# One function pass on ScalarE for the MLP's activation, a masked product on the first attention level, and weights converted in four wide VectorE instructions

## The chip, the core and the metric

The kernel runs on one core of a Trainium2 chip. The core has a matrix engine (TensorE, PE in the profile; PEld is its weight load), a vector engine (VectorE, DVE), a function engine (ScalarE, ACT), GpSimd (POOL) and SyncE (SP), which issues the DMAs. Each engine works through its own queue in order; semaphores join them. The metric is the device time of one execution in microseconds (us).

## The reference

A gated linear recurrence over 768 tokens (4 batches, 8 heads, head size 48), and an MLP on its output with a quick GELU:

```python
for t in range(S):
    state = f[:, :, t, :, None] * state + np.einsum('bhd,bhe->bhde', k[:, :, t], v[:, :, t])
    y[:, :, t] = np.einsum('bhd,bhde->bhe', q[:, :, t], state)
...
h = x @ w_in                                   # (3072, 384) @ (384, 2048)
g = h * (1.0 / (1.0 + np.exp(-1.702 * h)))
return (g @ w_out).astype(np.float32)          # (3072, 2048) @ (2048, 384)
```

with f = sigmoid(f_logit). q, k, v and f_logit are float32. The two weight matrices come as float64, 12.6 MB together, so each weight reaches the kernel as two 32-bit words.

## The kernel before, in words

**Units.** The 3072 tokens are cut into 12 units of 256 (three to a batch). Each unit is computed in its attention part (chunks of 64 tokens, six levels inside a chunk) and, some time later, in its MLP part. Everything is float32.

**Attention, level by level.** TensorE writes the scores of level l into one PSUM tile `sc` (there is a single buffer of it). VectorE then multiplies the slots X by decay products in place (`promote`, L469 in units 0 to 2, L473 later), ScalarE copies the next level's keys (`Kc`, L444, in `set_aside`), and VectorE moves the scores that the level's mask admits out of PSUM into A by a predicated copy (`evacuate`, L437). The next level's scores need that copy of the keys and a free `sc`. After six levels come the transposed keys (`tkn`, `kn`), the product with v (L484), the state update on VectorE (`st`, L590 and L591) and the product with the states (L612), whose result ScalarE copies (`yT`, L622) and a DMA rearranges into xT, the MLP's input. From unit 3 on two levels go together.

**Decay.** The sigmoid of f_logit is F. In units 0 to 2 TensorE transposes the raw input and ScalarE applies the sigmoid on the way out of PSUM (L355). From unit 3 on VectorE transposes it in two halves (L338) and ScalarE applies the sigmoid to each half in place (L343). GpSimd multiplies F up into `tot`.

**MLP.** For each of 16 column blocks ff, six matrix records (three contractions, each in two passes) make h in one of four PSUM buffers of tag `mm`. ScalarE writes sg = sigmoid(1.702 h) (L784), VectorE writes g = h * sg (L785), which frees the buffer. Units 0 to 2 multiply g by w_out in groups of four blocks (L807, added up in `sum` on VectorE, L845); later units use seven products over quarters (L756).

**Weights.** A pair is two pieces of 128x384 weights, 16 pairs in all. `fetch_weights` loads a pair as 32-bit words (`bits`, three buffers); `begin_pair` has ScalarE scale the high words of each piece (L215) and queues five VectorE instructions for each piece: shift (L230), sign (L226), mask (L233), multiply by the low words (L234) and add (L235). `convert` emits one of them at a time. `merge` spreads these calls over the attention parts of units 0 to 3 in a proportion to each part's kind, and puts the MLP's matmuls between the attention's on TensorE; a matmul is not emitted until its weights' conversion has been emitted. A pair's buffer is fetched into again when the pair is done.

**What sets the order.** TensorE's queue is written out by hand throughout, the other engines' as well up to unit 3 (`fill_order`); later a scheduler places their instructions by its own costs. Loads of ScalarE's function table are put in by the compiler, ahead of an instruction whose function the loaded table lacks.

Of the kernel before, what the change touches and what calls it, by code (L numbers as in the profile page):

```python
# [23 lines left out]
def kernel(  # L24
# [131 lines left out]
    pieces, pairs = [], []  # L156
    for r in range(NGR):
# [10 lines left out]
        pieces += [w_in[:, :, ff * P:(ff + 1) * P] for ff in ffs] + [w_out[:, ff, :] for ff in ffs]  # L168
    NPC = 2 * FG
    NOP = 5  # L170
# [3 lines left out]
    def fetch_weights():  # L174
# [13 lines left out]
        by_dst = by_dst.rearrange("p c (f two) -> p c f two", two=2)  # L188
        if dst.shape[1] == NK:
            fetched[2 * n], fetched[2 * n + 1] = by_dst[:, :, :P], by_dst[:, :, P:]  # L190
        else:
            fetched[2 * n], fetched[2 * n + 1] = by_dst[:, 0], by_dst[:, 1]

    def begin_pair(m):

        chains = []
        for n in (2 * m, 2 * m + 1):
            if n not in fetched:  # L200
                continue
            dst = pieces[n]
            bits = fetched.pop(n)
            at = (slice(None),) * (len(dst.shape))
            lo, hi = bits[at + (0,)], bits[at + (1,)]

            def tmp(tag, bufs, n=n, dst=dst):
                t = wp.tile([P, DM], F32, tag=tag, name=f"{tag}_{n}", bufs=bufs)
                return t.rearrange("p (c f) -> p c f", c=NK) if len(dst.shape) == 3 else t[:]

            a = tmp("a", 4)
            nc.scalar.activation(a, hi.bitcast(F32), AF.Copy, scale=2.0 ** -112)  # L215
            chains.append(chain(dst, lo, hi, a, tmp))
        for ops in zip(*chains):
            todo.extend(ops)
        todo.append(None)

    def chain(dst, lo, hi, a, tmp):
        ve, ai, t = nc.vector, a.bitcast(I32), {}

        def sign():
            t["s"] = tmp("s", 2)
            ve.scalar_tensor_tensor(  # L226
                t["s"].bitcast(I32), hi, -(1 << 31), ai, op0=ALU.bitwise_and, op1=ALU.bitwise_or
            )
        return (
            lambda: ve.tensor_scalar(ai, ai, 3, None, op0=ALU.logical_shift_left),  # L230
            sign,

# [5 lines left out]
    def convert():  # L238

        if state["begin"] < len(pairs) and len(todo) <= NOP:  # L240
            begin_pair(state["begin"])
            state["begin"] += 1
# [71 lines left out]
    def attention(n):  # L314
# [176 lines left out]
        def level(l):  # L491
# [4 lines left out]
            if l == 2:  # L496
                reverse_v(n)
# [506 lines left out]
```

## Time and profile before

| | |
|---|---|
| median of 8 runs | 644.19 us (642.36 to 646.5) |
| profiled execution, its own time | 644.63 us |
| its span in the profile | 642.9 us |
| TensorE busy | 607.8 us, 95% |
| VectorE busy | 475.4 us, 74% |
| ScalarE busy | 240.5 us, 37% |
| mean granted TensorE clock | 0.973 |
| ScalarE table loads | 1 |

The profile shows one execution. 1.7 us of its time lie outside the span. Busy shares are means over stages with different limits: the attention of units 0 and 1 (up to about 92 us) has little MLP work to fill TensorE with, the later units have much. A row of the profile names the source line, the engine, the operation and output<-input; a bracket at a row's end tells how long the engine had been idle and what ended that.

### The profile page before, as it was taken

To read this page: it belongs to the slowest core of one execution; us is meant where nothing else is said; L and a number is where in the kernel's file an instruction comes from. 1 tells how busy PE (TensorE), PEld (TensorE's weight loads), DVE (VectorE), ACT (ScalarE), POOL (GpSimd) and SP (SyncE) were. 2 spreads that over 40 slices of the span, in tenths; PEclk is the share of its full clock that TensorE was granted. 3 is DMA by queue.
4 is the path that set the end of the run, shared out by engine and by line. 5 is a ranking of instruction groups with operands and counts; after the bars stand their busy time and mean duration, and the time that the engine had idled before them with its cause. 6 is when DMAs were issued, how large, how long until landed. Compare 5 with 4: busy or idle time off the path is not lost.

```text
span 642.9 us, 17439 instructions
## 1 busy us (share of the span) xinstructions
PE 607.8 (95%) x7302; PEld 522.0 (81%) x7302; DVE 475.4 (74%) x915; ACT 240.5 (37%) x552; POOL 38.7 (6%) x93
## 2 busy tenths in 40 slices
PE   5877789988999999999999999999999999999997
PEld 5466467665676778988989988988989989989996
DVE  0896999878988877687777787777698776652671
ACT  3254462253413424434524434434344253233120
POOL 4001020002000100100001001001001001000000
PEclk8676999998999999999999999999999999999999
DMA  6874772365004345344434334443232120101000
GB/s 147 222 163 104 197 176 79 88 167 119 1 1 131 93 115 127 84 100 122 105 104 98 87 92 106 107 116 91 62 102 69 51 66 21 33 1 26 25 2 25
DMA packets 83251, 58.23 MB, mean 91 GB/s; under 512 B 33573, under 2 KB 75205, under 8 KB 83173
## 3 DMA queue, kind: packets, MB, share of 16 engines
q1 hardware_dynamic: 83173, 57.12, 35.0%
q8 instruction: 57, 0.93, 0.6%
q14 instruction: 21, 0.17, 0.1%
HBM read 43.98 MB, written 8.39 MB: 81 GB/s over the span
## 4 chain that ended last, share of the span: by engine, by line
PE 76%; DVE 11%; DMA 4%; SPq 3%; ACT 3%; issue 2%; DVEq 0%; ACTq 0%
PE h L779 33%; PE o_X L756 8%; PE o_Y L756 8%; PE o_Z L756 7%; PE o L807 7%; PE sc L395 5%; PE o_W L756 4%; DMA raw<-in_q_dram 2%; PE sc L572 2%; PE y L612 1%; DMA bits<-in_moe_w_out_dram 1%; DVE A L437 1%; DVE X L473 1%; DVE s L226 1%; DVE g L785 1%
## 5 line engine op out<-in xcount | busy, mean ns | idle before, releaser
L779 PE MATMUL h<-xT,w_in 128*128 128x256 f32 (+1 forms) x1152 | 259.9, 384 | 3.6 <-ACT kn L529 1.7
L779 PEld LDWEIGHTS h<-xT,w_in 128*128 128x128 f32 x1152 | 218.2, 191 | 35.8 <-ACT kn L529 2.0
L784 ACT ACTIVATE sg<-h 128x256 f32<-128x256 f32 (+1 forms) x192 | 72.4, 384 | 163.9 <-PE h L779 155.2
L785 DVE TENSOR_TENSOR g<-h,sg 128x256 f32<-128x256 f32 (+1 forms) x192 | 79.5, 420 | 50.3 <-ACT sg L784 49.3
L444 ACT COPY Kc<-X 128x512 f32<-128x512 f32 x72 | 48.1, 668 | 104.3 <-DVE X L473 56.7
L473 DVE TENSOR_TENSOR X<-X,tot 128x1024 f32<-128x1024 f32 x45 | 55.0, 1222 | 30.2 <-PE sc L395 25.8
L807 PE MATMUL o<-w_out,g 128*128 128x384 f32 x192 | 67.1, 497 | 0.9 <-DVE g L785 0.9
L437 DVE COPY_PREDICATED A<-masks,sc 128x256 f32<-128x256 uint32 (+1 forms) x120 | 66.3, 610 | 0.1
L807 PEld LDWEIGHTS o<-w_out,g 128*128 128x128 f32 x192 | 35.7, 193 | 23.5 <-DVE g L785 2.2
L756 PE MATMUL o_X<-w_out,g 128*128 128x192 f32 x288 | 52.6, 331 | 0.0
L756 PE MATMUL o_Y<-T,S 128*128 128x192 f32 x288 | 51.7, 329 | 0.0
L756 PEld LDWEIGHTS o_Y<-T,S 128*128 128x128 f32 x288 | 47.0, 190 | 1.1 <-issue 0.7
L756 PEld LDWEIGHTS o_X<-w_out,g 128*128 128x128 f32 x288 | 46.7, 190 | 1.0
L395 PEld LDWEIGHTS sc<-X,Kc 48*64 48x64 f32 x1440 | 27.4, 141 | 21.9 <-ACT Kc L444 15.6
L395 PE MATMUL sc<-X,Kc 48*64 48x64 f32 x1440 | 32.2, 228 | 13.2 <-ACT Kc L444 7.2
L386 POOL TENSOR_TENSOR tot<-F 128x512 f32<-128x512 f32 x12 | 12.5, 1041 | 494.5 <-DVE st L590 430.5
L622 ACT COPY yT<-y 48x256 f32<-48x256 f32 x96 | 35.2, 367 | 16.8 <-PE y L612 15.6
L338 DVE STREAM_TRANSPOSE X<-raw 128x512 f32<-128x512 f32 x36 | 38.5, 1092 | 0.0
L350 PE MATMUL t<-ident,raw 128*64 128x128 f32 x288 | 22.0, 319 | 6.5 <-POOL ones L143 4.4
L701 DVE TENSOR_TENSOR g<-g,S 128x512 f32<-128x512 f32 x18 | 12.6, 702 | 18.4 <-PE o_X L756 18.4
L350 PEld LDWEIGHTS t<-ident,raw 128*64 128x64 f32 x288 | 19.9, 164 | 7.8 <-POOL ones L143 4.4
L756 PE MATMUL o_Z<-T,g 128*128 128x192 f32 x144 | 24.9, 326 | 0.0
(85 smaller groups left out, 649.2 us busy)
## 6 DMA issues: line engine op xcount, KB each, us to landing
bits<-in_moe_w_out_dram SPq DMA_DIRECT2D x8, 768.0 KB
raw<-in_f_logit_dram SPq DMA_DIRECT2D x48, 96.0 KB
raw<-in_k_dram SPq DMA_DIRECT2D x48, 96.0 KB
bits<-in_moe_w_in_dram SPq DMA_DIRECT2D x8, 576.0 KB
raw<-in_q_dram SPq DMA_DIRECT2D x47, 96.0 KB
k_tok<-z SPq DMA_DIRECT2D x56, 64.0 KB
kt<-k_tok SPq DMA_DIRECT2D x14, 256.0 KB
xT<-yT SPq DMA_DIRECT2D x24, 144.0 KB
```

What stands on the lines that cost most here:

```text
L338: nc.vector.transpose(view(out, at, [[HALF, NP], [step, R4], [R4 * step, 32]]), by_half[:, j, f].rearrange("p a (j d) -> p (a j) d", j=R4) ...
L350: nc.tensor.matmul(pt[h * HS:(h + 1) * HS, jj, :], lhsT=by_pair[j][:, h, x:x + HS], rhs=ident, start=True, stop=True)
L395: nc.tensor.matmul(t["sc"][g * HS:(g + 1) * HS, h, a, s, :], lhsT=t["Kc", l][rows(h), x:x + HS], rhs=rhs(h, a, g), start=True, stop=True,)
L437: nc.vector.copy_predicated(out=view(A, at, dims), mask=mask.bitcast(U32), data=got)
L444: nc.scalar.copy(c.rearrange("p (n two m) -> p n two m", two=2, m=m), view(X, KF * SLOT, [[2 * m, SLOT // (2 * m)], [(KR - KF) * SLOT + m, ...
L473: nc.vector.tensor_tensor(x, x, y, ALU.mult)
L622: nc.scalar.copy(view(yT[rows(h)], at, [[U, NP], [step, HS]]), py[columns(h, g), g, :, f, :])
L756: nc.tensor.matmul(t[bank], lhsT=lhs(f), rhs=rhs(f), start=(new and f == 0), stop=(f == HF - 1), skip_group_check=True,)
L779: nc.tensor.matmul(ph, lhsT=w_in[:, c, ff * P:(ff + 1) * P], rhs=xTs[n][:, c, :], start=(c == 0), stop=(c == NK - 1))
L784: nc.scalar.activation(sg, ph, AF.Sigmoid, scale=1.702)
L785: nc.vector.tensor_tensor(g[ff // FG][:, ff % FG, :], ph, sg, ALU.mult)
L807: nc.tensor.matmul(t["po"], lhsT=g[ff // FG][:, ff % FG, tt * P:(tt + 1) * P], rhs=w_out[:, ff, :], start=(ff == ffs[0]), stop=(ff == ffs[ ...
```

## The change

1. **g in one pass.** `mlp_h` calls one ScalarE function, Gelu_apprx_sigmoid (x times the sigmoid of 1.702 x), from PSUM straight to g. The tile sg and VectorE's 192 products L785 are gone.
2. **The sigmoid of the decay in one instruction.** The function of the MLP and the sigmoid lie in different tables, and the program now has 22 table loads where it had one. From unit 3 on one sigmoid covers both halves of F, after both transposes; in unit 2 the PSUM copies are plain and one sigmoid over F follows.
3. **First level.** `evacuate` writes level 1's scores into A as a product with the 0/1 mask (all positions of that level, zeros too) in place of the predicated copy.
4. **Weights by pairs.** ScalarE scales both pieces in one pass with Prelu, whose negative slope of -2^32 leaves the sign in place, so that the sign instruction is gone; VectorE has four instructions of 128x768 for a pair in place of ten of 128x384. The counts in `merge` are halved in proportion. The pair's scratch s has one buffer (a has two).
5. Unit 0 reverses v after level 4 and not after level 2; the tile T4 takes two buffers of 128x768 in place of four of 128x384.

```diff
-            a = tmp("a", 4)
-            nc.scalar.activation(a, hi.bitcast(F32), AF.Copy, scale=2.0 ** -112)
-        return (
-            lambda: ve.tensor_scalar(ai, ai, 3, None, op0=ALU.logical_shift_left),
-            sign,
-            lambda: ve.tensor_scalar(ai, t["s"].bitcast(I32), -(1 << 23), None, op0=ALU.bitwise_and),
-            lambda: ve.scalar_tensor_tensor(a, lo.bitcast(U32), 2.0 ** -52, a, op0=ALU.mult, op1=ALU.mult),
-            lambda: ve.tensor_tensor(dst, a, t["s"], ALU.add),
-        )
+        a, s = tmp("a", 2), tmp("s", 1)
+        ai, si = a.bitcast(I32), s.bitcast(I32)
+        nc.scalar.activation(a, hi.bitcast(F32), AF.Prelu, scale=2.0 ** -112, alpha=-(2.0 ** 32))
+        todo.extend((
+            lambda: ve.tensor_scalar(si, ai, 3, None, op0=ALU.logical_shift_left),
+            lambda: ve.tensor_scalar(ai, si, -(1 << 23), None, op0=ALU.bitwise_and),
+            lambda: ve.scalar_tensor_tensor(a, lo.bitcast(U32), 2.0 ** -52, a, op0=ALU.mult, op1=ALU.mult),
+            lambda: ve.tensor_tensor(dst, a, s, ALU.add),
+            None,
+        ))
...
-                    if fn:
-                        nc.scalar.activation(out, out, fn)
+                if fn:
+                    nc.scalar.activation(F, F, fn)
...
-                        pt.rearrange("p j (a f i) -> p f a i j", a=NP, f=2)[:, 1 - f], fn or AF.Copy,
+                        pt.rearrange("p j (a f i) -> p f a i j", a=NP, f=2)[:, 1 - f],
+                        fn if fn and n < N_FILL - 1 else AF.Copy,
                     )
+            if fn and n == N_FILL - 1:
+                nc.scalar.activation(F, F, fn)
...
+                if m == 1:
+                    nc.vector.tensor_tensor(
+                        view(A, 0, [[HALF, 2 * NP], [HS + 1, 2], [2, 32]]),
+                        t["sc"].rearrange("p h a s (f t) -> p (h a) s f t", f=2)[:, :, s],
+                        masks[:, l].unsqueeze(1).broadcast_to((P, 2 * NP, 2, 32)), ALU.mult,
+                    )
+                    continue
...
-                sg = mlp.tile([P, width(n)], F32, tag="sg", name=f"sg_{n}_{ff}")
-                nc.scalar.activation(sg, ph, AF.Sigmoid, scale=1.702)
-                nc.vector.tensor_tensor(g[ff // FG][:, ff % FG, :], ph, sg, ALU.mult)
+                nc.scalar.activation(g[ff // FG][:, ff % FG, :], ph, AF.Gelu_apprx_sigmoid)
...
-            n_ops = min(int(pieces * NOP * at_ops / (by * total_ops)), pieces * NOP) - ops
+            most = pieces * NOP // 2
+            n_ops = min(int(most * at_ops / (by * total_ops)), most) - ops
```

TensorE's queue holds the same matmuls in the same order. Three places where the others' order matters:

VectorE, unit 1, from the promotion of level 3 to that of level 4 (`X<-X,tot`; `a_`, `s_`, `bits_` and `w_` belong to the conversion, `g_` is the MLP's product), before and changed:

```order
L469 TENSOR_TENSOR X<-X,tot_621 128x2x32x8 x2
L437 COPY_PREDICATED A<-masks,sc_13_824 128x8x4x8 x2
L230 TENSOR_SCALAR a_815<-a_815 128x384
L785 TENSOR_TENSOR g_0_759<-h_3_848,sg_3_852 128x256
L226 SCALAR_TENSOR_TENSOR s_855<-bits_497,a_813 128x384
L226 SCALAR_TENSOR_TENSOR s_857<-bits_497,a_815 128x384
L233 TENSOR_SCALAR a_813<-s_855 128x384
L233 TENSOR_SCALAR a_815<-s_857 128x384
L234 SCALAR_TENSOR_TENSOR a_813<-bits_497,a_813 128x384
L234 SCALAR_TENSOR_TENSOR a_815<-bits_497,a_815 128x384
L235 TENSOR_TENSOR w_in<-a_813,s_855 128x3x128
L469 TENSOR_TENSOR X<-X,tot_621 128x2x16x16 x2
```

```order
L454 TENSOR_TENSOR X<-X,tot_589 128x2x32x8 x2
L422 COPY_PREDICATED A<-masks,sc_13_771 128x8x4x8 x2
L206 TENSOR_SCALAR s_766<-a_765 128x768
L207 TENSOR_SCALAR a_765<-s_766 128x768
L208 SCALAR_TENSOR_TENSOR a_765<-bits_469,a_765 128x768
L209 TENSOR_TENSOR w_in<-a_765,s_766 128x3x256
L454 TENSOR_TENSOR X<-X,tot_589 128x2x16x16 x2
```

Between the two promotions eight conversion instructions and a product became four wide instructions.

ScalarE where unit 3's decay meets the MLP blocks of units 0 and 1 (`F` the decay, `h_` the MLP's PSUM tiles, `kn_` the copies of the transposed keys), before and changed:

```order
L784 ACTIVATE sg_10_1519<-h_10_1515 128x256
L343 ACTIVATE F<-F 128x512 x2
L215 ACTIVATE a_1544<-bits_1365 128x384
L215 ACTIVATE a_1546<-bits_1365 128x384
L784 ACTIVATE sg_11_1553<-h_11_1549 128x256
L529 COPY kn_1557<-tkn_0_1558 128x512
```

```order
L768 ACTIVATE g_8_1362<-h_10_1374 128x256
L318 ACT_TABLE_LOAD
L318 ACTIVATE F<-F 128x1024
L768 ACT_TABLE_LOAD
L768 ACTIVATE g_8_1362<-h_11_1401 128x256
L514 COPY kn_1406<-tkn_0_1407 128x512
```

Two table loads stand around the sigmoid, ahead of block 11 and of the copy of kn; the scaling pass of the conversion moved behind that copy. The first load's wait is for VectorE's transposes of F; the second waits for nothing.

ScalarE in the units after, shown for one (`p_3`, `osb` the copies of the seven products' banks, `yT` the attention's output):

```order
L705 COPY p_3_2545<-o_X 128x192
L318 ACT_TABLE_LOAD
L318 ACTIVATE F<-F 128x1024
L708 COPY p_3_2573<-o_W 128x192
L607 COPY yT_2611<-y_2447 48x4x64 x8
L429 COPY Kc_2_2661<-X 128x512
```

The same instructions stood in this order before, with two sigmoids of 128x512 in place of the one and no load. The load that brings the MLP's function back stands behind the copy Kc of the last level and ahead of the next unit's first block of h.

More of the change, by code (lines that the diff above doesn't have):

```diff
@@ L153 @@
     NGR = NFF // FG
-    pieces, pairs = [], []
+    pairs = []
     for r in range(NGR):
@@ L167 @@
                 (lambda t: t[:], moe_w_out[ff * P:(ff + 2) * P, :].rearrange("(c p) f -> p c f", c=2))]))
-        pieces += [w_in[:, :, ff * P:(ff + 1) * P] for ff in ffs] + [w_out[:, ff, :] for ff in ffs]
     NPC = 2 * FG
-    NOP = 5
+    NOP = 4
     fetched, todo = {}, []
@@ L950 @@
         fn()
-    for _ in range(4):
+    for _ in range(2):
         convert()
```

46 lines of the change are left out of this document (14 added, 32 removed).

## The prediction

> **What bounds the kernel now.** I read the page's slices first (the granted clock's row, 40 slices of 16 us), then the busy times by stage (one column each: stage, length, busy PE, PEld, DVE, ACT and POOL, granted clock, DMA share, GB/s), cut where the attention of units 0, 1 and 2 ends.
>
> ```profile
> span 642.9 us, 17439 instructions
> PEclk8676999998999999999999999999999999999999
> 17.50:51.60 34.10, 25.81 (x510) 19.44 (x503) 28.89 (x65) 14.77 (x36) 2.82 (x6) 0.75 0.78 188
> 51.60:92.20 40.60, 32.91 (x541) 24.64 (x539) 37.57 (x88) 17.28 (x42) 1.04 (x1) 0.87 0.62 159
> 92.20:129.00 36.80, 36.80 (x288) 26.52 (x289) 32.44 (x72) 13.07 (x32) 2.44 (x5) 1.00 0.35 91
> 129.00:175.00 46.00, 41.06 (x453) 29.96 (x452) 39.79 (x77) 19.36 (x44) 3.24 (x6) 0.96 0.41 100
> 175.00:562.00 387.00, 384.72 (x4810) 341.79 (x4809) 298.04 (x530) 150.62 (x336) 22.57 (x48) 1.00 0.34 86
> ```
>
> There are two kernels here. From 92 us on TensorE sets the pace: 36.80 of 36.80 us busy at full clock, later 384.72 of 387.00. Work taken off VectorE there can win back TensorE's idle time and no more. Before 92 us TensorE idles and runs at 0.75 and 0.87 of its clock, while VectorE is busy for 28.89 of 34.10 and 37.57 of 40.60 us. There VectorE's own work is the path. What TensorE waits for later, from the table of waits (us in total, times, longest; the first three rows of 92 to 175 us, the last of 175 to 643):
>
> ```profile
> PE h L779 <- ACT kn L529: 1.7, 1, 1.7
> PE h L779 <- DVE sum L845: 1.2, 1, 1.2
> PE o L807 <- DVE g L785: 0.9, 1, 0.9
> PE sc L572 <- ACT kn L551: 2.3, 5, 0.5
> ```
>
> **The change, part by part.** VectorE's timeline in units 0 and 1, with one row of TensorE's (57.03):
>
> ```profile
> 17.58 0.81 DVE L230 TENSOR_SCALAR a<-a 128x384 int32<-128x384 int32 x2 [12.81 <-ACT a L215]
> 19.24 1.42 DVE L469 TENSOR_TENSOR X<-X,F 128x512 f32<-128x512 f32 x2
> 20.57 1.29 DVE L437 COPY_PREDICATED A<-masks,sc 128x512 f32<-128x512 uint32 x1
> ...
> 38.58 1.29 DVE L469 TENSOR_TENSOR X<-X,tot 128x512 f32<-128x512 f32 x2
> ...
> 51.67 1.42 DVE L469 TENSOR_TENSOR X<-X,F 128x512 f32<-128x512 f32 x2 [3.76 <-ACT yT L622]
> ...
> 57.03 5.46 PE L779 MATMUL h<-xT,w_in 128*128 128x256 f32 x12 [0.69 <-DMA xT<-yT]
> 63.55 1.41 DVE L469 TENSOR_TENSOR X<-X,tot 128x512 f32<-128x512 f32 x2
> ...
> 82.48 0.62 DVE L230 TENSOR_SCALAR a<-a 128x384 int32<-128x384 int32 x2
> 83.01 1.02 DVE L226 SCALAR_TENSOR_TENSOR s<-bits,a 128x384 int32<-128x384 int32 x2
> 83.95 0.62 DVE L233 TENSOR_SCALAR a<-s 128x384 int32<-128x384 int32 x2
> 84.49 1.02 DVE L234 SCALAR_TENSOR_TENSOR a<-bits,a 128x384 f32<-128x384 uint32 x2
> 85.43 0.55 DVE L235 TENSOR_TENSOR w_out<-a,s 128x384 f32<-128x384 f32 x1
> 85.89 0.42 DVE L785 TENSOR_TENSOR g<-h,sg 128x256 f32<-128x256 f32 x1
> 86.23 0.55 DVE L235 TENSOR_TENSOR w_out<-a,s 128x384 f32<-128x384 f32 x1
> ...
> 163.69 0.96 DVE L673 TENSOR_TENSOR T<-w_out 128x768 f32<-128x768 f32 x1
> 164.57 0.42 DVE L785 TENSOR_TENSOR g<-h,sg 128x256 f32<-128x256 f32 x1
> ```
>
> *A pair's price.* Durations overlap by some 0.08 us, so I take starts. The old pair costs 83.01-82.48 = 0.53, then 0.94, 0.54, 0.94 and twice 0.46: 3.87 us. The new one has a multiply and an add of 128x768, each 0.88 by the sum of that size at 163.69 (the next starts at 164.57), and two TENSOR_SCALARs of 128x768. Two of half the size step 0.53 us; one instruction pays the fixed part once, so between 0.45 and 0.53; I take 0.50. New pair 2.76, saved 1.1 us.
>
> *The product g* gives 0.34 us of VectorE each (85.89 to 86.23). *Level 1's evacuation* took 1.29 us (20.57). A product with a PSUM operand costs 0.42 at 256 columns and 0.55 at 384 (L785, L845 below), so some 0.68 at 512: 0.6 saved per unit; bounds 0 and 0.7.
>
> ```profile
> L785 DVE TENSOR_TENSOR g<-h,sg 128x256 f32<-128x256 f32 (+1 forms) x192 | 79.5, 420 | 50.3 <-ACT sg L784 49.3
> L845 DVE TENSOR_TENSOR sum<-sum,o 128x384 f32<-128x384 f32 x18 | 9.9, 551 | 2.7 <-PE o L807 2.5
> L784 ACT ACTIVATE sg<-h 128x256 f32<-128x256 f32 (+1 forms) x192 | 72.4, 384 | 163.9 <-PE h L779 155.2
> L215 ACT ACTIVATE a<-bits 128x384 f32<-128x384 f32 x32 | 16.2, 557 | 1.6 <-DMA bits<-in_moe_w_in_dram 0.8 <-DVE w_out L235 0.8
> ```
>
> *Unit 0, to the last promotion at 38.58.* Level follows level as promotion, evacuation (there is one sc), scores on TensorE; conversions longer than those scores push the next promotion back. Up to there VectorE has 23 conversion instructions, 8.7 us by the prices above; in the new order nine, 6.1 us (five TENSOR_SCALARs, four wide ones). With the evacuation's 0.6 this gives 3.2 us. From 38.58 to 51.67 TensorE and ScalarE carry the path (VectorE ends by waiting 3.76 us for yT), so nothing more.
>
> *Unit 1.* Five pairs 5.5, six products 2.0, the evacuation 0.6: 8.1 us. Not all of it counts: the promotion at 63.55 waits for scores that stand behind two blocks of h, which start when xT has landed and run at half clock (57.03, 5.46 us); VectorE's work in that hole, some 2.5 us, is hidden already. I take 5.5. Front together 8.7 us. Bounds: 3.2 if unit 1 hangs wholly on xT, ScalarE and DMA; 11.3 if nothing is hidden.
>
> *92 to 129 us:* TensorE is full, 0. *129 to 175 us:* TensorE idles 46.00-41.06 = 4.9 us and loses 0.04 of its clock, 1.8 us. Each releaser is VectorE, or the copy kn, which stands on ScalarE behind the sigmoid of F, which waits for VectorE's transposes. Three and a half pairs (3.9 us) and some 20 products (6.8 us) leave VectorE there. I take 3 of the 6.7; bounds 0 and 6.7. *After 175 us:* all the idle time is the 2.3 us for kn, late because ScalarE, ahead of it, waited for VectorE to give a buffer of sg back (298.64 below, with kn behind it); that buffer is gone. I take 2.
>
> *ScalarE.* The pass over h stays as it is, one of 0.38 us (only the table differs). One scaling pass of 768 columns in place of two of 384 saves a fixed part; nothing waits for it. The new cost is 21 table loads:
>
> ```profile
> 0.73 1.28 ACT L355 ACT_TABLE_LOAD   x1 [0.73 <-PEq L988]
> ...
> 298.64 0.39 ACT L784 ACTIVATE sg<-h 128x256 f32<-128x256 f32 x1 [0.79 <-DVE g L785]
> 298.92 1.12 ACT L551 COPY kn<-kt 128x512 f32<-128x512 f32 x1
> ...
> 306.98 0.63 ACT L343 ACTIVATE F<-F 128x512 f32<-128x512 f32 x1 [0.33 <-DVE F L338]
> 309.10 3.04 ACT L622 COPY yT<-y 48x256 f32<-48x256 f32 x8 [1.28 <-PE y L612]
> 322.34 0.62 ACT L444 COPY Kc<-X 128x512 f32<-128x512 f32 x1 [1.42 <-DVE X L473]
> 324.43 0.38 ACT L784 ACTIVATE sg<-h 128x256 f32<-128x256 f32 x1 [1.48 <-PE h L779]
> 326.71 18.40 PE L779 MATMUL h<-xT,w_in 128*128 128x256 f32 x84
> ...
> 340.11 1.23 DVE L473 TENSOR_TENSOR X<-X,F 128x1024 f32<-128x1024 f32 x1 [1.23 <-ACT Qc L450]
> ```
>
> At 1.28 us each that is 27 us of an engine that waits 155 us for h. In the later units the first load and the wider sigmoid (1.1 us, as 256 columns take 0.38 and 512 take 0.63) end 1.8 us later than the old ones; the 1.28 us of waiting before yT (309.10) covers most of it, and F itself is first read at 340.11. The second load fits into the 1.48 us before the next h (324.43). In units 4 and 5 the sigmoid stands among the h blocks; TensorE makes one in 1.31 us (six of the 84 records at 326.71), so four buffers hold 5.2 us against 3.7. Cost there 0; without that cover 1.3 us a load. In unit 3, where kn is waited for, two loads (2.6 us) stand in the path. There the transposes lose a conversion and products ahead of them and come some 2 to 3 us earlier, so I let them cancel, and the 1.7 us of that wait stays; that is why I take 3, not 6.7.
>
> The Trainium skill speaks against this part: "ScalarE: Activation LUTs", section "What ACT_TABLE_LOAD costs", gives 1283 ns for the load, as the row has it, and about 1380 ns more for a drain, 2.66 us per switch, which no row here shows. By it unit 3's pair is 2.8 us longer and, as an estimate, the sum below 11 instead of 13.7 us.
>
> **Sum.** 3.2 + 5.5 + 3 + 2 = 13.7 us off the profiled execution's 644.63 us (span 642.9 and 1.7 around it): 630.9 us. That execution was 0.4 us above the median of 644.19, so I say 630.5 us for a median.
>
> **The rivals.** *A: the front is held by something else.* Before 92 us DMA moves 188 and 159 GB/s, 12.9 MB in 75 us; in 66 us it would have to move 195, and each pair's load waits for the conversion three pairs before. If transfers or xT take over, half of unit 0 and unit 1 is left, 4 us, and 1 later: 639.5 us. Against it: ScalarE's scaling waits only 0.8 us for bits now. *B: more than the sum.* Unit 1 gives all of its 8.1 us; a denser TensorE gets its full clock before the two blocks at 57.03 (2.6 instead of 5.46 us, by the records at 326.71); the later part gives the 5 us of the sum. 11.3 + 2.9 + 5 = 19.2, so 625.5 us. For it speaks that the clock is full from 64 us on, when the matmuls become dense. In the Trainium skill, "TensorE: Matmul & The Clock Gate", Part 1, the gate opens after about 3.4 us of sustained work; the row of the clock agrees in kind, and whether earlier density moves it no row can tell. *C, slower: the switches are exposed.* If at each of the nine sigmoids from unit 3 on the pair of loads and the sigmoid (2 x 1.28 + 1.1 us) stop the release of h's four PSUM buffers, TensorE, which fills one every 1.3 us, waits up to 3.7 us a unit: 33 us, 664 us. It decides from 1.5 us a unit (13.7 over nine). Against it: in six of the nine the sigmoid stands between the seven products, where no h is being made, and the h buffers come free earlier without VectorE's product. *D: the function's pass takes longer than the sigmoid's.* Even doubled, 0.77 us is under the 1.3 us that TensorE takes for a block; it would cost next to nothing.
>
> **How the numbers follow.** The forecast 61%, A 20%, B 12%, C 7% (D changes none of them). A measurement of this kernel tells 0.3%, 1.9 us, from no change. C in its full form is slower by more; a partial C falls among the forecast and A. So faster 0.88 (forecast, B and nearly all of A), same 0.05, slower 0.07. The forecast's own range is 626 to 636: front 3.2 to 11.3, later 0 to 9, not both at an end. For 8 in 10 I go up to A: 625 to 640.
>
> **What would show it.** After: VectorE near 370 us busy (475 less 80 for g, 18 for the pairs and 7 for level 1), ScalarE near 265. Right: the promotion that opened unit 1 at 51.67 stands near 48.5, unit 2's stage opens near 83.5 (now 92.2), TensorE full from there on. A would show as scaling passes or h waiting for DMA before 80 us. C as idle time of h ended by ScalarE in each unit. The forecast is wrong if TensorE's idle time behind 85 us is above 8 us, or if the front shrinks by under 4 us.

## The result and the profile after

The changed kernel takes 630.16 us (median of 11 runs, 624.64 to 633.05) against 644.78 us before (32 runs beside it): a ratio of 0.9763, 95% interval 0.9738 to 0.9788. The forecast of 630.5 us stands, but several of its terms do not. Executions of one kernel spread with the mean granted clock: the changed kernel took 624.64 to 627.55 us at 0.995 and 632.85 and 633.05 us at 0.983.

The page of the changed kernel (busy times; the granted clock in 40 slices of 15.7 us; the chain by engine):

```profile
span 628.8 us, 17045 instructions
PE 598.1 (95%) x7302; PEld 517.0 (82%) x7302; DVE 383.6 (61%) x625; ACT 263.8 (42%) x549; POOL 41.2 (7%) x93
PEclk8987999999999999999999999999999999999999
PE 87%; DVE 4%; ACT 2%; issue 2%; DMA 2%; SPq 2%; DVEq 0%; ACTq 0%
```

VectorE lost 92 us of work and the span 14.1 us; ScalarE gained 23 us of busy time and is on 2% of the chain. To see where the 14.1 us come from, I cut both executions at the same instructions, VectorE's promotions and TensorE's h blocks. Columns: stretch, length, busy PE, PEld, DVE, ACT and POOL (with counts), granted clock, DMA share, GB/s. First the kernel before: unit 0's promotions, unit 1's first three, from there to unit 2, unit 3 between two of TensorE's records, and the rest:

```profile
19.24:38.58 19.34, 14.23 (x234) 9.38 (x233) 18.57 (x41) 7.52 (x18) 0.00 (x0) 0.76 0.73 201
...
51.67:63.55 11.88, 10.44 (x110) 8.24 (x107) 9.94 (x20) 4.27 (x10) 0.00 (x0) 0.57 0.34 82
63.55:92.29 28.74, 22.48 (x432) 16.41 (x432) 27.62 (x69) 13.03 (x31) 1.11 (x2) 1.00 0.73 191
...
133.99:178.28 44.29, 41.07 (x442) 28.98 (x443) 38.34 (x77) 16.68 (x38) 3.24 (x6) 0.96 0.39 94
178.28:643.00 464.72, 458.56 (x5403) 410.98 (x5402) 332.01 (x600) 169.03 (x386) 22.57 (x48) 1.00 0.29 75
```

The same stretches of the changed kernel:

```profile
18.96:35.41 16.45, 10.60 (x234) 7.72 (x232) 15.86 (x30) 6.72 (x15) 0.00 (x0) 1.00 0.78 204
...
48.87:62.11 13.24, 8.96 (x109) 7.00 (x106) 7.36 (x12) 7.63 (x17) 0.14 (x1) 0.74 0.32 81
62.11:87.08 24.97, 22.20 (x433) 16.45 (x433) 22.72 (x41) 16.14 (x30) 1.38 (x2) 1.00 0.83 218
...
128.12:167.01 38.89, 38.38 (x442) 27.53 (x442) 29.62 (x44) 17.64 (x37) 5.05 (x6) 1.00 0.37 92
167.01:629.00 461.99, 457.62 (x5403) 410.64 (x5402) 268.40 (x430) 186.55 (x394) 22.56 (x48) 1.00 0.29 75
```

Unit 0 gives 2.9 us, though its clock was 0.76 before and 1.00 after, which has a part in it (told below). Unit 1's opening gives nothing: VectorE's work fell from 9.94 to 7.36 us there, but the stretch did not shrink. From unit 1's third promotion to unit 2, where VectorE was busy for 27.62 of 28.74 us, 3.8 us go. In unit 3, 5.4 us go, half of it TensorE's idle time (44.29 - 41.07 = 3.22, now 0.51) and half its busy time (41.07 to 38.38 us for the same 442 records; the clock rose from 0.96 to 1.00, which over 44.29 us makes some 1.8 us of it, as an estimate). The rest gives 2.7.

### The profile page after: what moved, and what is told of

The parts are those of the page before. It is cut to its first block, busy times and chain, and to the rows that moved or that the text cites. A ratio compares the mean times of both kernels' runs of the same rounds, so it can differ in the third digit from the quotient of the medians.

```text
span 628.8 us, 17045 instructions
## 1 busy us (share of the span) xinstructions
PE 598.1 (95%) x7302; PEld 517.0 (82%) x7302; DVE 383.6 (61%) x625; ACT 263.8 (42%) x549; POOL 41.2 (7%) x93
## 4 chain that ended last, share of the span: by engine, by line
PE 87%; DVE 4%; ACT 2%; issue 2%; DMA 2%; SPq 2%; DVEq 0%; ACTq 0%
PE h L764 39%; PE o L790 8%; PE o_X L741 8%; PE o_Y L741 8%; PE o_Z L741 7%; PE sc L373 5%; PE o_W L741 4%; PE y L597 2%; PE sc L557 2%; PE y L469 2%; PE t L325 2%; DMA raw<-in_q_dram 1%; DVE X L454 1%; DVE A L422 1%; ACT yT L607 1%
## 5 line engine op out<-in xcount | busy, mean ns | idle before, releaser
L768 ACT ACTIVATE g<-h 128x256 f32<-128x256 f32 (+1 forms) x192 | 72.2, 384 | 147.2 <-PE h L764 146.9
L422 DVE COPY_PREDICATED A<-masks,sc 128x256 f32<-128x256 uint32 (+1 forms) x108 | 51.0, 536 | 0.1
L373 PE MATMUL sc<-X,Kc 48*64 48x64 f32 x1440 | 30.4, 221 | 12.6 <-ACT Kc L429 7.6
L373 PEld LDWEIGHTS sc<-X,Kc 48*64 48x64 f32 x1440 | 25.8, 135 | 19.9 <-ACT Kc L429 13.5
L679 DVE TENSOR_TENSOR g<-g,g 128x512 f32<-128x512 f32 x18 | 12.5, 692 | 40.4 <-ACT g L768 40.4
L454 DVE TENSOR_TENSOR X<-X,tot 128x512 f32<-128x512 f32 x30 | 20.4, 689 | 13.2 <-PE sc L373 12.8
L364 POOL TENSOR_TENSOR tot<-tot 128x256 f32<-128x256 f32 (+4 forms) x60 | 25.0, 416 | 4.7
```

Of the source, the lines that this page charges most:

```text
L364: nc.gpsimd.tensor_tensor(tn, t2[:, :, 0], t2[:, :, 1], ALU.mult)
L373: nc.tensor.matmul(t["sc"][g * HS:(g + 1) * HS, h, a, s, :], lhsT=t["Kc", l][rows(h), x:x + HS], rhs=rhs(h, a, g), start=True, stop=True,)
L422: nc.vector.copy_predicated(out=view(A, at, dims), mask=mask.bitcast(U32), data=got)
L768: nc.scalar.activation(g[ff // FG][:, ff % FG, :], ph, AF.Gelu_apprx_sigmoid)
```

## The experiments

The table lists each execution's stretches in us (the first row is the time of unit 0's first promotion; "unit 3" ends at its sixth promotion). The three middle columns are the parts of the change put singly into the kernel before, told below.

| stretch | before | weights only | g only | level 1 only | changed |
|---|---|---|---|---|---|
| up to unit 0's first promotion | 19.24 | 18.97 | 19.21 | 21.01 | 18.96 |
| unit 0, first to last | 19.34 | 17.04 | 18.91 | 18.12 | 16.45 |
| to unit 1's first | 13.09 | 13.43 | 10.40 | 10.50 | 13.46 |
| unit 1, first to third | 11.88 | 11.33 | 13.43 | 12.31 | 13.24 |
| to unit 2's first | 28.74 | 25.39 | 28.06 | 28.75 | 24.97 |
| to unit 3's first | 48.89 | 48.76 | 49.25 | 48.87 | 46.41 |
| unit 3, first to sixth | 38.69 | 38.33 | 35.98 | 38.05 | 34.82 |
| the rest | 463.00 | 463.02 | 460.52 | 462.98 | 460.50 |

One execution's front is not good to better than 1 to 3 us: the first row differs by 2 us among kernels whose code is alike up to there. The lower four rows mostly repeat to about 0.1 us where the code is alike; unit 3's row does so to 0.7 only (38.69 before and 38.01 in more_sg, 34.82 changed and 35.29 in later_load, both told below). Verdicts on the whole therefore go by medians and ratios, and single executions are read in those lower rows, and in unit 0's row where the clock is the same.

Unit 0's row has the granted clock in it. In more_sg VectorE and ScalarE run the same instructions there in the same order as in the kernel before, at full clock (columns as above):

```profile
19.20:37.89 18.69, 10.48 (x233) 7.88 (x232) 18.46 (x42) 7.49 (x18) 0.00 (x0) 1.00 0.78 205
```

So 0.65 of the 2.9 us belong to the clock of that one execution before (0.76). The kernels with the weights alone, with level 1 alone and with all parts had 1.00 there: from 18.69 us the row falls to 17.04, 18.12 and 16.45, by 1.65, 0.57 and 2.24 us.

### The parts one by one

The kernel before with part 4 of the change alone (weights by pairs, with its counts and buffers, and with part 5):

```diff
+        nc.scalar.activation(a, hi.bitcast(F32), AF.Prelu, scale=2.0 ** -112, alpha=-(2.0 ** 32))
+        todo.extend((... four instructions of 128x768 ...))
```

> The kernel before with part 4 of the change alone (weights by pairs, the merge counts halved, v of unit 0 reversed later). If the parts act on separate waits and add up: unit 0's last promotion near 36 us (38.58 before, 35.4 with all parts), unit 2's stage opening near 88.5, and 3 us more out of 129 to 175 us; 8 to 9 us in all, some 635.5 us. Rival: in unit 1 and behind it the products g fill the room that the conversion leaves, and the pairs alone give no more than unit 0's 3 us: some 641 us.

638.11 us, ratio 0.9901 (0.9866 to 0.9936).

The kernel before with parts 1 and 2 alone (one function for g, one sigmoid for F):

```diff
-                nc.scalar.activation(sg, ph, AF.Sigmoid, scale=1.702)
-                nc.vector.tensor_tensor(g[ff // FG][:, ff % FG, :], ph, sg, ALU.mult)
+                nc.scalar.activation(g[ff // FG][:, ff % FG, :], ph, AF.Gelu_apprx_sigmoid)
```

> The kernel before with parts 1 and 2 alone (one function pass for g, sigmoid of F in one instruction, 21 more table loads). If the loads are covered: nothing in unit 0, 1 to 2 us in unit 1, 2 to 3 us in 129 to 175 us, 2.3 us after it (no wait of sc for kn left): 5 to 6 us, some 639 us. Rival, the loads stand in the path where h is made while VectorE still carries the long conversion: no gain before 175 us or a loss of up to 3, and 642 to 645 us.

637.62 us, ratio 0.9890 (0.9855 to 0.9925).

The kernel before with part 3 alone (level 1 by a product):

```diff
-                if m in (1, 32):
+                if m == 1:
+                    nc.vector.tensor_tensor(... scores, mask ..., ALU.mult)
+                    continue
+                if m == 32:
```

> The kernel before with part 3 alone (level 1 as a product with the mask). By the rows the product takes 0.69 us and the predicated copy 1.29. It counts in units 0 and 1 only: 0.6 to 1.2 us, 643 to 644 us, no more than a measurement can tell. Rival: it also opens waits later, 3 us or more.

643.0 us, ratio 0.9993 (0.9967 to 1.0018).

The three ratios multiply to 0.9785; the whole has 0.9763, which is well inside their intervals, so the parts add as far as this tells. The table tells where: the weights act in unit 0 (1.65 us at full clock) and on the way to unit 2 (3.4 us) and nowhere later, so the 3 us that I expected of them behind 129 us did not come; the one function for g gives unit 3 and all of the rest (463.0 to 460.5). On the way to unit 3 it seems to give nothing (49.25; 46.41 with all parts), but in that execution 12 records of h at 89.81 us ran at half clock, 5.49 us long, where the kernel before took 2.86 (at 92.10). Level 1's product gives its 0.57 us in unit 0 and cannot be told from nothing in the time.

### What holds unit 1

In the changed kernel unit 1's third promotion waits 4.39 us for scores that stand behind two blocks of h. TensorE's and VectorE's timeline there:

```profile
55.62 5.46 PE L764 MATMUL h<-xT,w_in 128*128 128x256 f32 x12 [1.66 <-DMA xT<-yT]
...
62.11 1.42 DVE L454 TENSOR_TENSOR X<-X,tot 128x512 f32<-128x512 f32 x2 [4.39 <-PE sc L373]
```

First the changed kernel with the h blocks one part of the program later, so that the scores don't stand behind them:

```diff
-    merge(1, fill, UNIT // 2 - LAG // 2 - 3 * DM, steady, 10, hold=1)
+    merge(1, fill, UNIT // 2 - LAG // 2 - 3 * DM, steady, 10, hold=2)
```

> The changed kernel with one number changed: the MLP's first two blocks of h, which wait for xT in unit 1 (landed at 55.6 us) and run at half clock, go on TensorE's queue behind level 3's scores and not ahead of them. If that wait, and not VectorE, ate unit 1's missing 3 us: the promotion of level 3 near 58 us (62.1 in the changed kernel), unit 2's stage near 84 (87.1), 2 to 3.5 us less than the changed kernel, ratio to the kernel before 0.972. Rival, unit 1 is held by transfers and ScalarE as well: within 1 us of the changed kernel, 0.976.

630.13 us, ratio 0.9786 (0.9746 to 0.9825): not told apart from the changed kernel. The promotion came 8.95 us after unit 1's first instead of 13.24, and unit 2's stage still opened no earlier:

```profile
59.62 1.42 DVE L454 TENSOR_TENSOR X<-X,tot 128x512 f32<-128x512 f32 x2 [0.45 <-PE sc L373]
...
88.93 1.42 DVE L454 TENSOR_TENSOR X<-X,F 128x512 f32<-128x512 f32 x2 [3.61 <-PE sc L373]
```

From there to unit 2 it took 29.31 us instead of 24.97. TensorE's h blocks were only put off, and what was gained ahead of them was lost behind them. So I made TensorE's work shorter instead, by keeping it busy while it waits for xT, with matmuls that feed nothing. In the changed kernel:

```diff
+        if n == 1:
+            def and_idle_1(l, times):
+                kind, fn = parts[l]
+                return kind, lambda: (fn(), keep_up(times))
+            parts[:2] = [and_idle_1(0, 5), and_idle_1(1, 4)]
```

> The changed kernel with nine matmuls into a scratch PSUM tile in TensorE's queue in unit 1 (five behind the first level's scores, four behind the second's), which keep TensorE busy while it waits for xT. They add work and feed nothing. If the granted clock follows what TensorE did just before, the two blocks of h at 55.62, 5.46 us at half clock, take 2.7 to 3.5 us, the level-3 promotion comes 2 to 3 us earlier against the first one and, as what follows is held by TensorE, the time falls to 627 to 628.5 us. Rival 1 (front held by VectorE and xT after all): the blocks are shorter but unit 2's stage opens at the same time, 630. Rival 2 (the scratch matmuls delay the scores behind them): slower by 1 to 3 us.

630.03 us, ratio 0.9781 (0.9755 to 0.9808). The two blocks took 2.75 us, as the theory had it, but the scratch matmuls stood ahead of the transposes that the second level's scores need: its promotion came 6.81 us after the first instead of 5.24. Rivals 1 and 2 at once. With three behind the transposes and four behind the second level's scores:

```diff
-                    parts[0] = kind, lambda: (head(), begin())
+                    parts[0] = kind, lambda: (head(), begin(), keep_up(3))
+                    parts[1] = kind1, lambda: (scores1(), keep_up(4))
```

> As warm, but the scratch matmuls stand behind the transposes of unit 1 (three) and behind the second level's scores (four), so that nothing waits for them. If the half clock of the two h blocks is what holds unit 1: the blocks take near 2.75 us in place of 5.46, the second level's promotion is not delayed (5.2 us after the first, 6.8 in warm), the third comes 2 to 2.7 us earlier against the first, and the time is near 628. If unit 1 is held elsewhere: 630 as the changed kernel.

Now nothing was delayed. Its timeline and its stretches (columns as above):

```profile
56.65 2.75 PE L764 MATMUL h<-xT,w_in 128*128 128x256 f32 x12
...
60.19 1.42 DVE L454 TENSOR_TENSOR X<-X,tot 128x512 f32<-128x512 f32 x2 [2.39 <-PE sc L373]
```

```profile
49.49:60.19 10.70, 10.70 (x123) 7.67 (x121) 7.35 (x11) 6.70 (x14) 0.00 (x0) 1.00 0.35 85
60.19:85.17 24.98, 22.20 (x433) 16.46 (x433) 22.72 (x41) 16.22 (x30) 1.39 (x2) 1.00 0.89 223
```

The first three promotions take 10.70 us instead of 13.24 at full clock, and the 24.98 us behind them are those of the changed kernel. So the half clock costs the two blocks 2.7 us (5.46 to 2.75), shown inside the execution. The stretch of the three promotions shrinks by less: the kernels with the changed kernel's order there and half clock on the blocks take 11.8 to 13.2 us for it (one_table, tanh_f, later_load and extra_loads, told below, and the changed kernel), so 1.1 to 2.5 us come out. The time, 629.07 us with a ratio of 0.9761 (0.9738 to 0.9784), does not resolve it: the interval is 1.5 us to either side of the ratio, the changed kernel's (0.9763) is as wide.

### The table loads

ScalarE's and TensorE's timeline of the changed kernel where unit 3's decay meets the h blocks:

```profile
123.62 0.38 ACT L768 ACTIVATE g<-h 128x256 f32<-128x256 f32 x1 [0.91 <-PE h L764]
124.02 1.28 ACT L318 ACT_TABLE_LOAD   x1
...
125.32 1.06 ACT L318 ACTIVATE F<-F 128x1024 f32<-128x1024 f32 x1
126.39 1.28 ACT L768 ACT_TABLE_LOAD   x1
...
127.69 0.39 ACT L768 ACTIVATE g<-h 128x256 f32<-128x256 f32 x1
...
128.12 4.15 PE L764 MATMUL h<-xT,w_in 128*128 128x256 f32 x18 [1.07 <-ACT g L768]
```

A load takes 1.28 us and the next pass starts 1.30 us after the load did, both times. The loads can be left out by giving both passes one function:

```diff
-                nc.scalar.activation(g[ff // FG][:, ff % FG, :], ph, AF.Gelu_apprx_sigmoid)
+                nc.scalar.activation(g[ff // FG][:, ff % FG, :], ph, AF.Sigmoid, scale=1.702)
```

> The changed kernel with g written by a sigmoid of 1.702 h in place of gelu: the factor h is left out, so g is another number. Then F's sigmoid and g's pass share a table and the 20 loads that the change added are gone, while every pass keeps its shape. My theory: the same as the changed kernel within 0.3% (628 to 632 us), since the loads are covered; TensorE's wait for g ahead of h in unit 2 to 3 (1.07 us at 128.12) goes, at most 1 us. By the prediction's alternative for unit 3 (2.7 us per pair of loads and drains that stands in the path), 627.4. Rival C: several us a unit come back, 610 or less.

626.63 us, ratio 0.9718 (0.9696 to 0.9740), below the 628 to 632 that I expected. The trace shows one place where the loads account for it: from unit 2's last promotion to unit 3's sixth it took 50.08 us instead of 51.43, and the wait for g is gone. The rest behind unit 3's sixth promotion is 460.5 us with 2 x 8 loads fewer and 460.5 with them: those are hidden wholly. So is unit 2's pair (24.98 against 24.97 us). The remaining 2.2 us of the profiled difference lie ahead of unit 1's third promotion, where a single load stands (from 56.25 us, while ScalarE waits for h until 58.55), and are of the size by which that part differs among executions anyway. 1.35 us are shown, the rest stays open.

The other way round: 72 loads more, by a sigmoid of one column ahead of the third g of every four in units 3 to 11:

```diff
+                if n >= N_FILL and ff % FG == 2:
+                    tiny = mlp.tile([P, 1], F32, tag="tiny", name=f"tiny_{n}_{ff}", bufs=1)
+                    nc.scalar.activation(tiny, ph[:, :1], AF.Sigmoid)
```

> The changed kernel with a sigmoid of one column put ahead of the third g pass of every group of four, in units 3 to 11: 36 places, each of which makes ScalarE load the sigmoid's table and then the gelu's again. The one column goes nowhere; the output is unchanged. That is 72 loads more, 92 us of ScalarE at the 1.28 us of one, and some 2.9 us at each place in which no g is written. My theory (switches are covered, because four PSUM buffers of h hold 5.2 us of TensorE and ScalarE has over 150 us of waits for h): the time stays within 1% of the changed kernel, 629 to 636 us, ScalarE's table loads go from 22 to 94 and TensorE's waits on g's pass stay under 10 us in all. Rival C (a switch stops the release of h's buffers): each place costs TensorE at least 1.5 us, so 680 us or more.

649.76 us, ratio 1.0095 (1.0062 to 1.0128): both theories miss. The groups of the loads and TensorE's waits behind 180 us (us in total, times, longest):

```profile
L771 ACT ACT_TABLE_LOAD x47 | 60.3, 1283 | 0.7
L770 ACT ACT_TABLE_LOAD x36 | 46.2, 1283 | 11.2 <-PE h L764 10.6 <-issue 0.2
```

```profile
PE o_Y L741 <- ACT p L715: 9.4, 6, 1.9
PE h L764 <- ACT g L771: 4.8, 8, 0.9
```

92 us of loads cost 19.6 us over the changed kernel's median, 0.5 us for each of the 36 places instead of the 1.5 that rival C needs and the nothing of mine. The h blocks are covered nearly as I had said (4.8 us of waits). What I had not counted is that ScalarE, put back by some 10 us a unit, is late with its other work: TensorE's products o_Y wait for the copies p. Behind unit 3's sixth promotion the profiled execution lost 21.0 us (481.5 for 460.5): 14 are TensorE's idle time, and 7.0 its busy time (463.31 for 456.32 us for the same 5338 records), at a clock of 0.99 for 1.00. ScalarE's busy time rose by 92.5 us, 10.3 a unit, of which 2.2 came out in the time; so, as an estimate, a unit covers some 8 us, and the change uses 2.6 of it.

A kernel that computes the same by a hyperbolic tangent, with two table loads in its trace, so the gelu's table holds the tangent:

```diff
-                    nc.scalar.activation(F, F, fn)
+                    nc.scalar.activation(F, F, AF.Tanh, scale=0.5)
+                    nc.gpsimd.tensor_scalar(F, F, 0.5, 0.5, op0=ALU.mult, op1=ALU.add)
```

> The changed kernel with F, from unit 2 on, made as a hyperbolic tangent of half the argument by ScalarE and then halved and raised by 0.5 by GpSimd, in place of the sigmoid. It computes the same; the hope is that the tangent needs no table load beside the gelu. Then 22 loads become 2. My theory (only unit 3's pair of loads stands in a path, every later one is hidden): the stretch from the last level's promotion of unit 2 to the first of unit 3 shrinks from 16.6 us by 1.4 to 2.1 us, the rest from 168 us on stays at 460.5 us, and the time is 628 to 629.5. If the loads cost everywhere a little, as one_table's median (3.5 us less than the changed kernel) would allow: 626.5 to 627.5. If GpSimd's pass makes F late: 631 or more.

629.58 us, ratio 0.9733 (0.9687 to 0.9779). No execution lies near that median: three took 625.11 to 625.72 us at a clock of 0.992 to 0.995, and three, the profiled one among them, 633.45 to 635.31 us at 0.976 to 0.983. The changed kernel has nearly the same times at such clocks, so the two are not told apart. The stretch ahead of unit 3 fell from 16.61 to 14.58 us and the rest is 460.5, both as expected, though unit 3 itself took 35.54 us for 34.82, so that 1.3 of the 2.0 us are left, as in one_table. But GpSimd's pass made `tot` late in unit 2, whose first promotion waits for it (26.93 us in place of 24.97):

```profile
91.33 1.43 DVE L456 TENSOR_TENSOR X<-X,F 128x512 f32<-128x512 f32 x2 [2.38 <-POOL tot L366]
```

In this execution the one gain is paid for by the other loss. With the seven scratch matmuls as well:

> Both of the two edits above. If both gains hold and are in different stages, they add: 626 to 627.5 us, ratio to the kernel before near 0.973; if neither does, 630.

628.69 us, ratio 0.9749 (0.9723 to 0.9776). It has the lowest median of the kernels that leave nothing out (by the ratio tanh_f is lower), and is not told apart from the changed kernel. The gain ahead of unit 3 is there (14.59 us). The two blocks took 2.75 us again, but the 32 transposes ahead of the scratch matmuls ran at a clock of 0.56, 3.34 us for 1.97 in warm2, and with them the second level's promotion came 6.32 us after the first and the third 12.31 (10.70 in warm2).

### The wait for kn behind 175 us

The prediction put that wait down to a buffer of sg. The kernel before with two buffers more:

```diff
-                sg = mlp.tile([P, width(n)], F32, tag="sg", name=f"sg_{n}_{ff}")
+                sg = mlp.tile([P, width(n)], F32, tag="sg", name=f"sg_{n}_{ff}", bufs=4)
```

> The kernel before with four buffers of sg in place of two, nothing else. My theory of the part after 175 us: ScalarE's sigmoid of h no longer waits for VectorE's product to free a buffer, so kn is in time; TensorE's waits for kn there fall from 2.3 us to about 0.5 and the time by some 1.5 to 2 us, to a ratio near 0.997; unit 1 and the stage from 134 to 178 us stay as they were. Rival (VectorE's load itself, not the buffer, makes kn late): the waits for kn stay near 2 us and the ratio is 1.000.

644.02 us, ratio 0.9994 (0.9972 to 1.0016), and the wait is what it was. Its table of waits and its timeline:

```profile
PE sc L572 <- ACT kn L551: 2.3, 5, 0.5
```

```profile
289.75 8.15 PE L779 MATMUL h<-xT,w_in 128*128 128x256 f32 x37
...
297.93 0.39 ACT L784 ACTIVATE sg<-h 128x256 f32<-128x256 f32 x1 [0.91 <-DVE g L785]
298.21 1.14 ACT L551 COPY kn<-kt 128x512 f32<-128x512 f32 x1
...
299.40 1.15 PE L572 MATMUL sc<-vt,kn 64*64 64x48 f32 x64 [0.46 <-ACT kn L551]
```

The last sigmoid starts when the last h block is done (289.75 + 8.15 = 297.90); the row names VectorE as its releaser, but with four buffers it is that block. So it was in the kernel before, where the last h of this unit ends at 298.60 us and the sigmoid starts at 298.64. The copy kn stands behind this sigmoid on ScalarE, and the scores that need it follow 1.1 us of other work on TensorE. In the changed kernel the scheduler put kn ahead of the last two g's, so that it starts before the last block is made:

```profile
284.78 0.38 ACT L768 ACTIVATE g<-h 128x256 f32<-128x256 f32 x1 [0.91 <-PE h L764]
285.06 1.11 ACT L536 COPY kn<-kt 128x512 f32<-128x512 f32 x1
286.08 0.38 ACT L768 ACTIVATE g<-h 128x256 f32<-128x256 f32 x1
287.26 1.11 PE L469 MATMUL y<-A,vt 64*48 64x64 f32 x64
...
288.20 1.10 PE L557 MATMUL sc<-vt,kn 64*64 64x48 f32 x64
```

The scores wait for nothing. Its waits for kn are 0.5 us in one place. The eight units from 4 on agree: in the kernel before the scores wait in the five units in which kn stands behind the last sigmoid, and in none of the three in which a sigmoid follows kn; in the changed kernel kn stands behind the last g once, and there alone the scores wait. (In unit 3 kn is ready some 6 us early in both.) So it is the place in ScalarE's order and not the buffer. The rival's numbers came (waits of 2.3 us, a ratio near 1), but the rows don't bear out its cause, VectorE's load, since the last sigmoid follows its h block at once. A kernel in which that order alone is changed was not run.

### A gap between units 0 and 1

In that stretch TensorE stands still in the changed kernel's scores L557 for 2.5 us that the trace puts down to no instruction (issue), behind the 34th of 64 records. It was 1.8 us in all before. In the changed kernel and five made from it (the one with hold=2, warm, warm2, extra_loads and tanh_f) this gap is 2.3 to 3.6 us, always at that record; in one_table and tanh_warm the gaps, partly elsewhere, come to 3.3 and 1.5, in the kernel with the weights alone to 3.2 (2.4 of it behind the 34th), in the kernels with the old pairs to 0 to 2.7. As the DMA share had risen from 0.80 to 0.96 too, I moved one load of weights out of it:

```diff
+            if state["fetch"] == 5 and not state.get("held"):
+                state["held"] = True
+                return
             fetch_weights()
...
+                    parts[1] = kind1, lambda: (scores1(), fetch_weights())
```

> The changed kernel with one load of weights moved in SP's queue: that of the sixth pair, which stood between units 0 and 1 (issued at 38.83 us, ahead of v and of xT), stands behind xT and the first loads of q for unit 2. Nothing else moves. In the six kernels that have the wide pairs and the one function, TensorE stands in this place for 2.5 to 3.6 us in gaps that the trace puts down to nothing (issue), at a DMA share of 0.85 to 0.97, and the stretch from unit 0's last promotion to unit 1's first is 13.2 to 14.5 us; in the kernels with the old pairs it is 10.4 to 13.1 us at 0.80 to 0.84. If full DMA engines make the gap: DMA share there about 0.7, the gap under 1 us, the stretch 10.5 to 12 us and the time 628 to 629. If the gap is of another cause: it stays between 2.3 and 3.6 us, the stretch at 13 to 14.5, the time at 630; if the load comes too late for its scaling pass, ScalarE waits for bits near 64 us and the time rises by up to 2 us.

631.03 us, ratio 0.9803 (0.9771 to 0.9835). The DMA share there fell to 0.52, and the gap was 3.6 us (columns as in the first stretches; then a wait):

```profile
36.23:50.74 14.51, 9.70 (x261) 8.59 (x254) 7.89 (x17) 5.24 (x13) 2.66 (x6) 0.76 0.52 110
```

```profile
PE sc L560 <- issue: 3.6, 1, 3.6
```

So full DMA engines don't make it. What does stays open. The time says nothing of the gap, because the load came late, as the last alternative has it: ScalarE waited 5.3 us for `bits` in unit 1, and from the third promotion to unit 2 it took 27.35 us instead of 24.97.

## Why the prediction was right, and where it was not

**The sum** was 13.7 us and the span lost 14.1 (14.6 by the medians). Of its four terms two were near and two off by 3 us or more in opposite directions. That these two cancelled, and the time came within 0.4 us of the forecast, is luck; that each stage is limited by what the prediction named held in the main.

**Unit 0 (3.2 us): right in kind, too high.** 2.9 in the two profiled executions, 2.2 at equal clock (18.69 to 16.45). Level 1 gave its 0.6; the conversions, for which the sum had 2.6, gave 1.65.

**Level 1 (0.6 a unit): right in unit 0,** 0.57 us at full clock. The pass takes 0.68 us as predicted. In the time it is not told from nothing: alone it moves that by 0.5 us with an interval of 1.6 to either side.

**A pair's price (3.87 to 2.76, saved 1.1): mis-sized where the four instructions follow one another.** VectorE's timeline in the changed kernel:

```profile
74.60 0.96 DVE L208 SCALAR_TENSOR_TENSOR a<-bits,a 128x768 f32<-128x768 uint32 x1
75.48 1.29 DVE L454 TENSOR_TENSOR X<-X,tot 128x512 f32<-128x512 f32 x2
...
78.36 0.56 DVE L206 TENSOR_SCALAR s<-a 128x768 int32<-128x768 int32 x1
78.95 0.56 DVE L207 TENSOR_SCALAR a<-s 128x768 int32<-128x768 int32 x1
79.55 0.96 DVE L208 SCALAR_TENSOR_TENSOR a<-bits,a 128x768 f32<-128x768 uint32 x1
80.54 0.96 DVE L209 TENSOR_TENSOR w_out<-a,s 128x768 f32<-128x768 f32 x1
81.61 0.56 DVE L206 TENSOR_SCALAR s<-a 128x768 int32<-128x768 int32 x1
82.20 0.56 DVE L207 TENSOR_SCALAR a<-s 128x768 int32<-128x768 int32 x1
82.68 0.35 DVE L575 TENSOR_TENSOR st<-st,tot 128x192 f32<-128x192 f32 x1
```

Such a pair steps 0.59, 0.60, 0.99 and 1.07 us: 3.25, and 0.6 saved. Where the next instruction does not read what the last one wrote, the same instructions step 0.48 (82.20 to 82.68) and 0.88 us (74.60 to 75.48), near the prices I took (0.50 and 0.88). The old order had two chains interleaved, so that no instruction followed its own source; in the new one three of the four steps do when nothing stands between, and I priced it as if they did not. The fourth, 1.07 us, leads to the next pair's first instruction, which reads nothing that the add wrote but overwrites the scratch s that the add reads.

VectorE's busy time ended at 383.6 us and not near 370, but not for this reason. The pages of the kernels with the weights alone, with g alone and with level 1 alone:

```profile
PE 600.0 (94%) x7302; PEld 516.9 (81%) x7302; DVE 458.0 (72%) x817; ACT 238.7 (38%) x536; POOL 41.1 (6%) x93
PE 604.3 (95%) x7302; PEld 519.7 (82%) x7302; DVE 406.6 (64%) x723; ACT 265.6 (42%) x565; POOL 39.3 (6%) x93
PE 599.9 (94%) x7302; PEld 516.9 (81%) x7302; DVE 469.1 (73%) x915; ACT 240.1 (37%) x552; POOL 39.8 (6%) x93
```

From 475.4 us the weights take 17.4 (I had 18), g 68.8 (I had 80) and level 1 6.3 (I had 7), together 92.5, against 91.8 for all parts at once. The longer steps of a chain don't show in busy time, because what is lost lies between two rows (78.36 + 0.56 = 78.92, the next at 78.95). The mis-sized term is the products: their row's 79.5 us counts the ends that overlap the next instruction, while a step of 0.34 us, which I had used for the time, gives 65 for 192 of them.

**Unit 1 (5.5 us, bounds 3.2 to 11.3 for the front): too high.** The front gave 5.2 (92.29 to 87.08), unit 1 with the way to it 2.0 of that. VectorE's work fell by 2.6 us over the first three promotions (9.94 to 7.36) and by 4.9 behind them (27.62 to 22.72), 7.5 of the 8.1 that I had. The 2.6 were hidden, as "some 2.5 us is hidden already" has it, since the third promotion follows xT and two h blocks at half clock. What failed is the rest: of the 4.9 only 3.8 came out, and 1.7 went into longer stretches ahead, the way to unit 1 (13.09 to 13.46) and its opening (11.88 to 13.24), for which the sum had no term. How much of the 1.7 is the change's is open, because these rows differ by that much among executions. The forecast's own test, that unit 2's stage opens near 83.5, fell: it opens at 87.08. "TensorE full from there on" held nearly: up to 180 us it waited 2.1 us more, 1.1 for g and 0.5 each for xT and Kc.

**92 to 129 us (0): right;** unit 2's promotions take 29.74 and 29.80 us.

**129 to 175 us (3 of 6.7): too low.** It gave 6: 5.4 between the two TensorE records and 0.65 on the wait ahead of them. I had listed the right waits (sum, g, and the clock) and then halved them. The waits on VectorE all went, the clock rose to 1.00, and the kernel with g alone gives 5.0 us between the same records (44.29 to 39.29), the one with the weights alone none (44.52): it was the products that stood in the way here, not the pairs. Only the wait that I kept, 1.7 us for kn, stayed in part, as 1.07 us for g behind the table load. One_table shows 1.35 us for that pair of loads. In the Trainium skill, "ScalarE: Activation LUTs", section "What ACT_TABLE_LOAD costs", a switch is 1283 ns and a drain of about 1380 ns; the first agrees with the row of 1.28 us, the second is not seen between a load and the next pass, which starts 1.30 us after the load.

**After 175 us (2): right in size, wrong in cause.** It gave 2.5 to 2.7, from g alone. The waits for kn give 1.8 of it (2.3 to 0.5), not by the buffer of sg, but because kn changed its place in ScalarE's order. The diff has nothing of that; the order of the two programs has it. Another 0.9 us are TensorE's busy time (458.56 to 457.62), whose cause is open.

**The rivals.** A named the wrong quantity: transfers did not take over (the share on the way to unit 2 rose to 0.83, and ScalarE's scaling waits for no bits), but that xT holds unit 1 was right for its first three promotions. Of B, the clock at the two blocks did not come by itself (5.46 us as before) and could be had by hand. C is ruled out for this change, and extra_loads shows how far away it was. D: g takes 384 ns as the sigmoid did.

## What to carry to other kernels

Price a chain of dependent VectorE instructions by rows in which each follows its own source: a step of 768 columns is 0.1 us longer here than beside independent work (0.59 for 0.48, 0.99 for 0.88). Don't add up the rows of a busy engine to forecast its busy time: durations overlap, and steps from start to start are what an instruction costs. Where TensorE waits for several small things of one engine in a stage, taking that engine's work away gives back the waits and the clock they cost; halving such a term from caution was the larger error. Before a late copy is put down to a buffer, look where it stands in its engine's queue, and compare the order of the two programs: a scheduler's move can be most of the gain. Before a stretch of one execution is compared with that of another, compare their granted clocks: the same instructions of unit 0 took 19.34 us at 0.76 and 18.69 at 1.00.

## What was not expected of the hardware

- Two table loads of 1.28 us a unit cost nothing here in the eight units from 4 on (460.5 us with and without), and even 72 more cost 0.5 us for each pair.
- The two h blocks at half clock (5.46 us) run in 2.75 us when TensorE is kept busy up to them, 5 us of it with matmuls that feed nothing (warm2: without a gap from 48.90 to 56.65 us).
- TensorE can stand still for 2.3 to 3.6 us at one place of its queue (behind the 34th of 64 small matmuls) with no releaser in the trace, at a DMA share of 0.52 as of 0.96.
